# Preparing DMA-transposed pairs on GpSimd, two pairs ahead, and storing 128 rows in one DMA

## The chip, the cores and the metric

The kernel runs on one core of one Trainium2 chip. The metric is the device time of one execution in microseconds (us). Before the change it is 434.28 us (median; 434.15 to 434.98). Times of a kernel and of the kernel before are taken in the same rounds on the same chip. Engine names in the profile: PE is TensorE's matmuls, PEld its weight loads, DVE is VectorE, ACT ScalarE, POOL GpSimd, SP SyncE; SPq is SP's sequencer, which issues DMAs. A DMA has landed when its data have arrived. Tile names: `kst`, `qst` and `vst` are K, the queries and V as loaded, `kc` the copied K, `qp` the summed queries, `kT` and `qT` their transposes, `psc` the scores, `er` their exponentials, `xn` and `xT` the attention's output and its transpose, `osb` rows of the result before they are stored.

## The reference, cut to what matters

```python
def _attn_ref(q, k, v):                       # (8, 8, 1152, 64) each
    q_pool = q.reshape(B, H, S // 2, 2, D).mean(axis=3)
    attn = softmax(q_pool @ k.T / sqrt(D))    # 576 pooled queries, 1152 keys
    return attn @ v
# x = (batch, query) rows x 512 columns, 4608 rows
def _moe_ref(x, w1, w2, w3, w_out):           # 512 -> 1024 -> 1024 -> 512
    return ((x @ w1) * (x @ w2) @ w3) @ w_out
```

The kernel treats two heads of one batch as a "pair": 32 pairs in all. Pooling is a sum of two neighbouring queries; the half goes into the softmax scale. The feed-forward part runs in nine units of 512 rows; seven of them are mixed into the attention loop, the last two make the tail.

## The kernel before

Pairs 0 to 7 are transposed by PE. From pair 8 on, K and the summed queries are transposed by DMA, two pairs at a time. Each such turn has five steps: six cast loads (fp32 to fp16, issued by GpSimd), two K copies, one sum of queries, one transpose of K and one of the queries (issued by SP), and then `settled`: two tiny GpSimd copies that read the transposed tiles, so that GpSimd issues the next six loads only after the transposes have landed.

```python
    def load_two(P):
        load_k(P)
        load_q(P)
        load_q(P + 1)
        load_k(P + 1)
        load_v(P)
        load_v(P + 1)

    def pool_q(P, n=1):
        # ... (tile qp, slices)
        nc.vector.tensor_tensor(
            out=qps[pp][r].rearrange("p c u d -> p u c d"),
            in0=src[:, :, :, 0, :], in1=src[:, :, :, 1, :], op=ALU.add)

    def prep_dma(P):
        for p in (P, P + 1):
            new_kq(p)
            nc.vector.tensor_copy(out=new_kc(p).rearrange("p j u d -> p u j d"), in_=kst.pop(p))
        nc.sync.dma_start_transpose(
            out=kTs[P // 2].rearrange("p t j f -> p (t j) f"),
            in_=kc2[P // 2].rearrange("p t j u d -> p (t j u d)"))
        pool_q(P, 2)
        nc.sync.dma_start_transpose(
            out=qTs[P // 2], in_=qps[P // 2].rearrange("p c u d -> p (c u d)"))

    def settled(P):
        for n, t in enumerate((kT[P], qT[P])):
            nc.gpsimd.tensor_copy(out=seen[:, n:n + 1], in_=t[0:1, 0, 0:1])
```

The end of a group of 128 output rows. The row of `out` for a query is `9 p + c`, because queries are kept in the order (c, p), with p from 0 to 63; so 64 rows of the tile `osb` go to 64 rows of `out` that lie nine rows apart:

```python
            def end(p):
                if s == 0:
                    osbs[i] = ffp.tile([128, dm], FP32, tag="osb", bufs=3, name="osb")
                # ... (DVE, in the tail ACT, writes osb from the PSUM tile p)
                for z in range(2):
                    b, f = divmod(t0 + 128 * i + 64 * z, SQ)
                    dst = out[b * SQ:(b + 1) * SQ, :].rearrange("(p c) m -> c p m", c=NJ)
                    eng = nc.scalar if final and z else nc.sync
                    eng.dma_start(out=dst[f // 64][:, cs], in_=osbs[i][64 * z:64 * z + 64, cs])
```

And the scheduler, where `at` is the position in the loop, counted in pairs:

```python
        elif prepped < NP and at >= prepped - 1.25:
            prep_dma(prepped)
            if loaded < NP:
                settled(prepped)
                load_two(loaded)
                loaded += 2
            prepped += 2
```

The softmax here doesn't subtract the row's maximum and nothing guards it: scores larger than these inputs give would overflow.

## Time and profile before

| of before | value | view |
|---|---|---|
| device time | 434.28 us | times |
| PE busy | 94% of the span | first part of the page |
| last exponential starts | 370.1 us | trace, start times of the exponentials |
| from there to the end (tail) | 63.3 us | span less the line above |
| step of the loads' turn | 23.85 us per two pairs | trace, issue times of the load groups |

The page first: busy time and share of each engine, PE's busy tenths, the granted TensorE clock in tenths, the packets of SP's queue, and the shares of the chain of waits that ended last, by engine and by line.

```profile
span 433.4 us, 12640 instructions
PE 408.2 (94%) x5432; PEld 270.3 (62%) x5432; DVE 211.2 (49%) x442; ACT 326.4 (75%) x355; POOL 78.4 (18%) x135
...
PE   3999999999996999799999999899999999999995
...
PEclk9999999999999899899999999999999999999999
...
q1 hardware_dynamic: 67968, 24.66, 31.4%
...
PE 72%; DMA 10%; ACT 6%; SPq 4%; DVE 3%; issue 2%; POOL 1%; DVEq 0%; POOLq 0%; ACTq 0%
PE po L276 16%; PE psc L251 15%; PE pa L369 14%; PE pb L369 13%; PE pp L387 10%; ACT er L261 6%; DMA vst<-in_v_dram 5%; DMA qT<-qp 4%; PE pT L353 3%; SPq L140 3%; DMA kst<-in_k_dram 1%; SPq L304 1%; DVE kc L139 1%; POOL kst L88 1%; DVE gT L381 1%
```

PE is dense: only three of 40 slices, at about 130, 174 and 270 us, drop below nine tenths outside the ends. The DMA issues of the same page (issuing engine, count, KB each, median us from issue to landing):

```profile
qst<-in_q_dram POOLq DMA_DIRECT2D x32, 288.0 KB, 7.2
vst<-in_v_dram POOLq DMA_DIRECT2D x32, 288.0 KB, 11.1
out_dram<-osb SPq DMA_DIRECT2D x70, 128.0 KB, 3.5
kst<-in_k_dram POOLq DMA_DIRECT2D x31, 288.0 KB, 8.0
```

The waits of the engines (engine, tile, line, what ended the wait: us in total, times, longest):

```profile
POOL seen L149 <- DMA kT<-kc: 193.4, 11, 22.6
ACT er L261 <- PE psc L251: 55.6, 99, 3.2
...
DVE osb L399 <- DMA out_dram<-osb: 6.8, 2, 6.2
...
PE psc L251 <- DMA qT<-qp: 4.7, 4, 3.3
```

GpSimd waits for the transposed kT for 193 of the 433 us, and nobody minds: it has nothing else to do. But it means that the next loads are not issued until the transposes are there. The timeline at 136 us (start, length, engine, line) shows a place where PE itself has to wait for a transpose:

```profile
134.03 1.40 SPq L144 DMA_TRANSPOSE qT<-qp  x1
...
137.69 0.09 PEld L251 LDWEIGHTS <-kT 64*128 64x128 f16 x1 [1.80 <-DMA kT<-kc]
137.77 0.18 POOL L149 COPY seen<-kT 1x1 f16<-1x1 f16 x1 [22.61 <-DMA kT<-kc]
139.44 0.66 PE L251 MATMUL psc<-qT,kT 64*128 64x256 f16 x6 [3.25 <-DMA qT<-qp]
```

### The profile page before, as it was taken

How to read it: one execution, taken by the hardware profiler on the slowest of the kernel's cores; microseconds unless marked ns; L12 is line 12 of the kernel's file. 1: busy time of each engine (PE TensorE's matmuls, PEld its weight loads, DVE VectorE, ACT ScalarE, POOL GpSimd, SP SyncE). 2: the span in 40 equal slices, each digit the busy share in tenths (PEclk: the TensorE clock that was granted, in tenths of full speed). 3: DMA queues.
4: the chain of work that ended last, by engine and by line, in shares of the span. 5: the costliest groups of instructions: out<-in, count | busy, mean ns of one | idle time of the engine just before them, and what ended most of it. 6: DMA issues, size and time to landing. Idle time of an engine off the chain costs nothing.

```text
span 433.4 us, 12640 instructions
## 1 busy us (share of the span) xinstructions
PE 408.2 (94%) x5432; PEld 270.3 (62%) x5432; DVE 211.2 (49%) x442; ACT 326.4 (75%) x355; POOL 78.4 (18%) x135
## 2 busy tenths in 40 slices
PE   3999999999996999799999999899999999999995
PEld 1677777766773577566775577466766776544442
DVE  1455565646453563456455544555465535613140
ACT  4898899889886688689878888788888888233332
POOL 8433331030401304030403012303004000000000
PEclk9999999999999899899999999999999999999999
DMA  8999999898776959995796979996968662050404
GB/s 126 205 208 201 180 193 188 157 165 119 124 171 95 170 79 161 223 164 110 119 188 111 150 127 205 169 165 118 223 119 133 97 138 36 14 114 1 98 0 98
DMA packets 94729, 59.16 MB, mean 136 GB/s; under 512 B 65360, under 2 KB 85072, under 8 KB 94672
## 3 DMA queue, kind: packets, MB, share of 16 engines
q0 software_dynamic: 26544, 33.56, 48.1%
q1 hardware_dynamic: 67968, 24.66, 31.4%
q8 instruction: 42, 0.69, 0.7%
q10 hardware_dynamic: 160, 0.13, 0.1%
q14 instruction: 15, 0.12, 0.1%
HBM read 67.11 MB, written 9.44 MB: 177 GB/s over the span
## 4 chain that ended last, share of the span: by engine, by line
PE 72%; DMA 10%; ACT 6%; SPq 4%; DVE 3%; issue 2%; POOL 1%; DVEq 0%; POOLq 0%; ACTq 0%
PE po L276 16%; PE psc L251 15%; PE pa L369 14%; PE pb L369 13%; PE pp L387 10%; ACT er L261 6%; DMA vst<-in_v_dram 5%; DMA qT<-qp 4%; PE pT L353 3%; SPq L140 3%; DMA kst<-in_k_dram 1%; SPq L304 1%; DVE kc L139 1%; POOL kst L88 1%; DVE gT L381 1%
## 5 line engine op out<-in xcount | busy, mean ns | idle before, releaser
L261 ACT ACTIVATE er<-psc 128x1024 f16<-128x1024 f32 x324 | 307.8, 1025 | 55.9 <-PE psc L251 55.6
L276 PEld LDWEIGHTS <-er 128*128 128x128 f16 x2880 | 105.2, 98 | 23.8 <-issue 7.3
L276 PE MATMUL po<-vt,er 128*128 128x65 f16 x2880 | 112.5, 194 | 0.4 <-DVE xn L293 0.4
L251 PE MATMUL psc<-qT,kT 64*128 64x512 f16 (+7 forms) x1152 | 98.0, 290 | 13.5 <-DMA qT<-qp 4.7
L369 PE MATMUL pa<-xT,w1sb 128*128 128x512 f16 x288 | 75.7, 386 | 0.0
L381 DVE TENSOR_TENSOR gT<-pb,asb 128x512 f16<-128x512 f32 x72 | 49.8, 692 | 52.8 <-PE pb L369 51.5
L369 PE MATMUL pb<-xT,w2sb 128*128 128x512 f16 x288 | 74.5, 381 | 0.0
L251 PEld LDWEIGHTS <-kT 64*128 64x128 f16 x1152 | 46.4, 95 | 39.3 <-issue 17.7
L387 PE MATMUL pp<-T,gT 128*128 128x256 f16 (+1 forms) x488 | 67.9, 292 | 0.0
L387 PEld LDWEIGHTS <-gT 128*128 128x128 f16 x488 | 45.7, 98 | 18.5 <-issue 3.7
L379 DVE COPY asb<-pa 128x512 f32<-128x512 f32 x56 | 38.7, 690 | 35.5 <-PE pa L369 34.4
L369 PEld LDWEIGHTS <-w2sb 128*128 128x128 f16 x288 | 26.6, 98 | 33.4 <-issue 5.0
L369 PEld LDWEIGHTS <-w1sb 128*128 128x128 f16 x288 | 25.3, 99 | 30.6 <-issue 6.8
L399 DVE TENSOR_SCALAR osb<-pp 128x256 f32<-128x256 f32 x49 | 20.8, 425 | 40.5 <-PE pp L387 33.4
L149 POOL COPY seen<-kT 1x1 f16<-1x1 f16 x11 | 2.0, 178 | 193.4 <-DMA kT<-kc 193.4
L289 DVE RECIPROCAL rz<-po 128x5 f32<-128x5 f32 x64 | 12.4, 194 | 49.0 <-PE po L276 48.6
L293 DVE TENSOR_TENSOR xn<-po,rz 128x320 f16<-128x320 f32 x64 | 31.5, 492 | 2.2
L88 POOL DMA_DIRECT2D kst<-in_k_dram x33 | 24.2, 733 | 10.9 <-DMA kst<-in_k_dram 3.2
L95 POOL DMA_DIRECT2D vst<-in_v_dram x32 | 23.3, 741 | 12.1 <-DVE vt L133 3.3
L396 ACT ACTIVATE osb<-pp 128x512 f32<-128x512 f32 (+1 forms) x12 | 7.0, 580 | 24.2 <-PE pp L387 24.2
L377 ACT COPY asb<-pa 128x512 f32<-128x512 f32 x16 | 9.4, 586 | 16.4 <-PE pa L369 16.4
L80 POOL DMA_DIRECT2D qst<-in_q_dram x32 | 19.5, 615 | 9.9 <-DMA xT<-in_moe_w_out_dram 2.1
(39 smaller groups left out, 135.5 us busy)
## 6 DMA issues: line engine op xcount, KB each, us to landing
qst<-in_q_dram POOLq DMA_DIRECT2D x32, 288.0 KB, 7.2
vst<-in_v_dram POOLq DMA_DIRECT2D x32, 288.0 KB, 11.1
out_dram<-osb SPq DMA_DIRECT2D x70, 128.0 KB, 3.5
kst<-in_k_dram POOLq DMA_DIRECT2D x31, 288.0 KB, 8.0
w3h<-in_moe_w_dram POOLq DMA_DIRECT2D x4, 512.0 KB, 14.9
xT<-in_moe_w_out_dram POOLq DMA_DIRECT2D x2, 512.0 KB, 14.2
w1sb<-in_moe_w_dram POOLq DMA_DIRECT2D x2, 512.0 KB, 16.2
w2sb<-in_moe_w_dram POOLq DMA_DIRECT2D x2, 512.0 KB, 17.2
```

The source lines that it names most:

```text
L80: nc.gpsimd.dma_start(out=qst[P // 2][o:o + 64].rearrange("p u t d -> p u (t d)"), in_=q[b, h0:h0 + 2].rearrange("u (p t) d -> p u (t d)", ...
L88: nc.gpsimd.dma_start(out=kst[P][:, :, js[0]:js[1], :], in_=k[b, h0:h0 + 2].rearrange("u (p j) d -> p u j d", j=NJ)[:, :, js[0]:js[1], :])
L95: nc.gpsimd.dma_start(out=vst[P].rearrange("p u j d -> p u (j d)"), in_=v[b, h0:h0 + 2].rearrange("u (p j) d -> p u (j d)", j=NJ))
L251: nc.tensor.matmul(t[:, u, o:o + ln].rearrange("p (c f) -> p c f", f=64), kT[P][s, j, :], qT[P][s, f0 // 64:(f0 + ln) // 64], start=True, ...
L261: nc.scalar.activation(out=er[:, :, r:r + CH], in_=psc.pop(c), func=AF.Exp, bias=0.0, scale=SCALE)
L276: nc.tensor.matmul(po[P, u][:, VW * x:VW * x + D + 1], er[:, u, r:r + 128], vts[P % 4][:, u, j, 0:D + 1], start=(m == 0), stop=(m == 44), ...
L293: nc.vector.tensor_tensor(out=xn[:, P % 2, :, u, :], in0=acc[:, :, 0:D], in1=rz.to_broadcast([128, 5, D]), op=ALU.mult)
L369: nc.tensor.matmul(p, w[:, mc, ft * 128:ft * 128 + 128], xT[:, mc, t0:t0 + 512], start=(mc == 0), stop=(mc == NC - 1))
L379: nc.vector.tensor_copy(out=asb[ft], in_=p)
L381: nc.vector.tensor_mul(out=gT[:, ft, :], in0=p, in1=asb.pop(ft))
L387: nc.tensor.matmul(p[:, 0:n], gT[:, ft, 128 * i:128 * i + 128], T16[:, ft, n * s:n * s + n], start=(ft == 0), stop=(ft == NF - 1))
L399: nc.vector.tensor_scalar_mul(out=osb, in0=p[:, 0:n], scalar1=1.0 / (SCL * SCL))
```

## The change

Its intent: take the K copies and query sums off DVE, whose in-order stream stalls when a load is late; prepare earlier, at 1.95 pairs ahead instead of 1.25, so that transposes never come late; and halve the number of store issues. The diff, with some unchanged lines and the two transposes shortened (`...`); the loads of K also move behind those of Q and V, and the copy of V moves a little (1.2 to 1.1):

```diff
     def load_two(P):
-        load_k(P)
         load_q(P)
         load_q(P + 1)
-        load_k(P + 1)
         load_v(P)
         load_v(P + 1)
+        load_k(P)
+        load_k(P + 1)
 
     def pool_q(P, n=1):
 
+        eng = nc.gpsimd if n == 2 else nc.vector
         ...
-        nc.vector.tensor_tensor(
+        eng.tensor_tensor(
 
     def prep_dma(P):
 
+        pool_q(P, 2)
         for p in (P, P + 1):
             new_kq(p)
-            nc.vector.tensor_copy(out=new_kc(p).rearrange("p j u d -> p u j d"), in_=kst.pop(p))
+            nc.gpsimd.tensor_copy(
+                out=new_kc(p).rearrange("p j u d -> p u j d").bitcast(mybir.dt.int32),
+                in_=kst.pop(p).bitcast(mybir.dt.int32))
         nc.sync.dma_start_transpose(... kT <- kc)
-        pool_q(P, 2)
         nc.sync.dma_start_transpose(... qT <- qp)
 
                 cs = slice(n * s, n * s + n) if final else slice(0, dm)
+                b, f = divmod(t0 + 128 * i, SQ)
+                if f < SQ - 64 and not final:
+                    dst = out[b * SQ:(b + 1) * SQ, :].rearrange("(p c) m -> c p m", c=NJ)
+                    nc.sync.dma_start(out=dst[f // 64:f // 64 + 2], in_=osbs[i])
+                    return
                 for z in range(2):
 
-        elif prepped < NP and at >= prepped - 1.25:
+        elif prepped < NP and at >= prepped - 1.95:
-        if copied < NP and at >= copied - (1.2 if copied >= NPE else 0.6):
+        if copied < NP and at >= copied - (1.1 if copied >= NPE else 0.6):
```

Of the 36 groups of 128 rows, 31 become one store: 21 before the last exponential and 10 in the tail. The merged store's destination has the shape 2 x 64 x 512, its source 128 x 512.

## The prediction

> **What bounds it now.** The page shows PE busy 94% of the span; the chain of waits is 72% PE. Until 372 us the matmul order is fixed by the program and repeats every 27 iterations (8 pairs); each iteration starts with three exponentials of ACT. Laying the start times of the exponentials of the repeats over each other, nearly all iterations agree within 0.05 us; six do not: about +5.0 us at 136 us, +3.9 at 177, +2.4 at 270, +0.9 at 164 and two smaller, together about 13 us. The timeline shows why: at 136 us PE waits for the DMA-transposed kT and qT (issued only at 131-134 us, behind xT transposes on the SP queue); at 174-178 and 267-272 us DVE, in order, waits in its K copy and V copy for kst and vst loads, and with it the evictions that PE needs. After the first two PE ran at half clock for 3.4 us (clock record; counted in the 13). Nothing else is to be had: from 372 us on it is a dense PE tail.
>
> **What the change does.** (1) 24 K copies (0.45 us each) and 12 query sums (0.75 us) leave DVE, which is no bottleneck (49%). On GpSimd, the Trainium skill (GPSIMD Engine Reference, section 3.1) has about 2.6 cycles per element at 1.2 GHz for a two-input op: estimate 2.5 us per sum, about 0.6-0.9 us per copy; this trace shows no such GpSimd op. POOL has room (18% busy). (2) Preparation comes 0.7 pair (about 8 us) earlier, so kT, qT have about 22 us instead of 14. The late kT/qT (+5.9 us) and the DVE blocks (+6.3 us) should go: -12 us, to about 422, if nothing else changed. (3) The loop loads -> copies -> transposes -> loads is serial: about 13 us from load issue to last landing plus about 8 us of transposes and issue; its 21-22 us barely fit in the 22.6 us of two pairs.
>
> (4) The stores. Before: 64 rows, 128 KB, 16 engines, 2 KB packets of 96 ns each, 3.5 us to landing. After: the destination's outermost dimension is 2 (2x64x512), the source's 128. The Trainium skill (DMA: Bandwidth & Descriptors, "Why a DMA increments its semaphore by 16 and not by 1") says the transfer runs on the largest number of engines up to 16 that divides both outermost sizes: here 2. No trace yet shows it. Then a store is 64 packets on each of two engines: about 6 us, and stores serialize there. Estimate: 31 of them, 180-190 us on those two engines, which also carry a sixteenth of every load and transpose (about 8.5 + 5 us per two pairs). In a 46 us unit (4 stores) they need about 48 us: near saturation. Loads and transposes finish with their slowest engine, and transposes queue behind stores, so the loop of (3) lengthens: I guess +5 to +35 us before 372 us. Tail: four stores per 20.7 us, three buffers; ACT waits for a buffer (+3 to +5 us), and the last three stores, made 1.7 us apart, drain in about 18 us: end +11 us.
>
> **Sum.** -12 +15 (tail) +10 = 448 us; range 424 to 470. Faster by 2%: 0.18; within: 0.25; slower: 0.57.
>
> **What would show it.** Store landing 7 us or more (before 3.5); a wait of the tail's osb for out_dram; a chain ending in out_dram; the gaps of 136, 174 and 267 us gone; DVE busy down about 20 us; GpSimd sum near 2.5 us; kT/qT waits near the bursts of stores.
>
> **What would make it wrong.** If the stores use 16 engines, expect about 422 us (faster). If two engines have spare capacity, only the tail pays: about 436. If transposes stick behind stores, over 470.

## The result

The changed kernel takes 513.48 us (median; 513.17 to 518.54). Its time is 1.1847 times that of before, with a 95% interval of 1.1773 to 1.1921. A ratio here is always the mean time of one kernel's fast runs over that of the other's fast runs of the same rounds, so it is not quite the ratio of the medians quoted. The direction was predicted; the size was not: 513 lies far outside 424 to 470.

The page after, the same lines as above:

```profile
span 511.1 us, 12544 instructions
PE 425.4 (83%) x5432; PEld 276.5 (54%) x5432; DVE 197.0 (39%) x406; ACT 326.1 (64%) x355; POOL 122.5 (24%) x171
...
PE   4999999998895999493998849489996969979870
...
PEclk9999999999899899988899969879997989989995
...
q1 hardware_dynamic: 67038, 24.65, 35.9%
...
DMA 39%; PE 38%; SPq 7%; ACT 5%; POOL 5%; issue 3%; DVE 1%; POOLq 0%; DVEq 0%; ACTq 0%
DMA kst<-in_k_dram 20%; DMA out_dram<-osb 12%; PE pb L372 8%; PE pa L372 8%; PE psc L254 8%; PE po L279 8%; SPq L144 6%; DMA qT<-qp 5%; ACT er L264 5%; PE pT L356 3%; POOL vst L95 2%; POOL qst L80 2%; PE pp L390 2%; DMA kT<-kc 1%; POOL kc L141 1%
```

PE's row now has holes (the first wait of over 1.5 us is at 126 us), and the chain has turned from PE (72% to 38%) to DMA (10% to 39%). Two of its links have grown most: the loads of K, from 1% to 20%, and the stores, from less than 1% to 12%. PE's busy time rose by 17 us with the same 5432 matmuls; the clock record has ten stretches at half clock between 129 and 457 us, 61 us together, each beginning in a wait of PE or within 2 us of its end. The Trainium skill, "TensorE: Matmul & The Clock Gate", table in "Part 1: The HAM clock gate (the "warmup" mystery)", puts half clock after an idle window of about 3.4 us. The longest waits of PE here are longer than that (9.2 us, in the list below), so I read the lower clock as a consequence of the waits, not as their cause. With the same program and 64-row stores (first experiment) the mean clock is 0.999; with nothing but idle work added to that (e12_loop5), which makes PE wait, it falls to 0.970.

The line of q1 is the most useful of the page. SP's queue moved the same bytes in 67968 - 67038 = 930 packets fewer. Nothing moved to GpSimd was on that queue; only the stores changed. The Trainium skill, "DMA: Bandwidth & Descriptors", section "Why a DMA increments its semaphore by 16 and not by 1", says that each engine which takes part in a store posts one increment of its own. Before, 31 pairs of stores posted 31 x 2 x 16 = 992 of these. 992 - 930 = 62 are left, which is 2 for each merged store. The records of single packets agree: 4-byte packets on this queue fell from 3456 to 2526, and of the 2 KB packets never more than two were in flight for 188 of the 207 us in which there were any (before, more than eight for 30 of 64 us). So a merged store does run on two engines. In the tail three stores, 384 packets, took 16.9 us, thus 5.6 us a store; the prediction had estimated 6.

The issues and the waits after:

```profile
qst<-in_q_dram POOLq DMA_DIRECT2D x32, 288.0 KB, 6.9
vst<-in_v_dram POOLq DMA_DIRECT2D x32, 288.0 KB, 11.1
kst<-in_k_dram POOLq DMA_DIRECT2D x31, 288.0 KB, 15.0
out_dram<-osb SPq DMA_DIRECT2D x31, 256.0 KB
```

```profile
ACT er L264 <- PE psc L254: 116.3, 100, 8.8
POOL kc L141 <- DMA kst<-in_k_dram: 88.2, 22, 11.1
POOL seen L152 <- DMA kT<-kc: 70.0, 11, 13.0
POOL qp L121 <- DMA qst<-in_q_dram: 60.2, 12, 13.5
...
DVE osb L402 <- DMA out_dram<-osb: 42.5, 6, 9.9
...
PE psc L254 <- DVE osb L402: 26.0, 5, 9.2
...
DVE xn L296 <- DMA xT<-xn: 18.8, 3, 8.8
```

ACT waits 61 us longer for scores. PE waits five times for DVE, which waits six times for one of the three `osb` tiles to be stored (42.5 us; before 6.8). One of these places in the timeline:

```profile
239.60 0.66 POOL L141 COPY kc<-kst 128x576 int32<-128x576 int32 x1 [5.77 <-DMA kst<-in_k_dram]
242.23 0.42 DVE L402 TENSOR_SCALAR osb<-pp 128x256 f32<-128x256 f32 x1 [9.55 <-DMA out_dram<-osb]
242.36 0.66 POOL L141 COPY kc<-kst 128x576 int32<-128x576 int32 x1 [2.10 <-DMA kst<-in_k_dram]
242.71 0.61 PE L254 MATMUL psc<-qT,kT 64*128 64x128 f16 x4 [8.74 <-DVE osb L402]
...
243.05 2.71 SPq L144 DMA_TRANSPOSE kT<-kc  x1
243.25 1.41 PEld L390 LDWEIGHTS <-gT 128*128 128x128 f16 x8 [0.41 <-issue]
243.25 1.89 PE L390 MATMUL pp<-T,gT 128*128 128x256 f16 x8
243.41 1.02 ACT L264 ACTIVATE er<-psc 128x1024 f16<-128x1024 f32 x1 [7.63 <-PE psc L254]
```

Read it from the inner end: DVE idles 9.55 us for a store, PE 8.74 us for DVE, ACT 7.63 us for PE, and in the same stretch GpSimd waits for its K loads, so the K transpose is issued late, at 243 us.

Where the time is. The last exponential starts at 431.0 us (before 370.1), so 61 us of the difference lie in the loop; the tail is 80.1 us (before 63.3), 16.8 us more.

### The profile page after: what moved, and what is told of

It reads as the page before. It is cut to its first block, busy times and chain, and to the rows that moved or that the text cites. A ratio compares the mean times of both kernels' runs of the same rounds, so it can differ in the third digit from the quotient of the medians.

```text
span 511.1 us, 12544 instructions
## 1 busy us (share of the span) xinstructions
PE 425.4 (83%) x5432; PEld 276.5 (54%) x5432; DVE 197.0 (39%) x406; ACT 326.1 (64%) x355; POOL 122.5 (24%) x171
## 3 DMA queue, kind: packets, MB, share of 16 engines
q1 hardware_dynamic: 67038, 24.65, 35.9%
## 4 chain that ended last, share of the span: by engine, by line
DMA 39%; PE 38%; SPq 7%; ACT 5%; POOL 5%; issue 3%; DVE 1%; POOLq 0%; DVEq 0%; ACTq 0%
DMA kst<-in_k_dram 20%; DMA out_dram<-osb 12%; PE pb L372 8%; PE pa L372 8%; PE psc L254 8%; PE po L279 8%; SPq L144 6%; DMA qT<-qp 5%; ACT er L264 5%; PE pT L356 3%; POOL vst L95 2%; POOL qst L80 2%; PE pp L390 2%; DMA kT<-kc 1%; POOL kc L141 1%
## 5 line engine op out<-in xcount | busy, mean ns | idle before, releaser
L279 PE MATMUL po<-vt,er 128*128 128x65 f16 x2880 | 114.9, 196 | 22.3 <-DVE xn L296 14.1
L279 PEld LDWEIGHTS <-er 128*128 128x128 f16 x2880 | 107.1, 99 | 41.2 <-DVE xn L296 18.1
L254 PE MATMUL psc<-qT,kT 64*128 64x512 f16 (+7 forms) x1152 | 102.1, 300 | 30.9 <-DVE osb L402 26.0
L372 PE MATMUL pb<-xT,w2sb 128*128 128x512 f16 x288 | 78.9, 397 | 10.6 <-issue 6.4
L254 PEld LDWEIGHTS <-kT 64*128 64x128 f16 x1152 | 47.7, 97 | 66.7 <-issue 46.8
L372 PE MATMUL pa<-xT,w1sb 128*128 128x512 f16 x288 | 78.0, 395 | 0.0
L390 PE MATMUL pp<-T,gT 128*128 128x256 f16 (+1 forms) x488 | 71.6, 303 | 0.0
L390 PEld LDWEIGHTS <-gT 128*128 128x128 f16 x488 | 47.4, 101 | 21.4 <-issue 5.3
L402 DVE TENSOR_SCALAR osb<-pp 128x256 f32<-128x256 f32 x49 | 20.6, 424 | 76.2 <-DMA out_dram<-osb 42.5
L121 POOL TENSOR_TENSOR qp<-qst 128x1152 f16<-128x1152 f16 x12 | 28.2, 2354 | 60.2 <-DMA qst<-in_q_dram 60.2
L296 DVE TENSOR_TENSOR xn<-po,rz 128x320 f16<-128x320 f32 x64 | 31.5, 492 | 20.9 <-DMA xT<-xn 18.8
L141 POOL COPY kc<-kst 128x576 int32<-128x576 int32 x24 | 15.8, 662 | 88.2 <-DMA kst<-in_k_dram 88.2
## 6 DMA issues: line engine op xcount, KB each, us to landing
vst<-in_v_dram POOLq DMA_DIRECT2D x32, 288.0 KB, 11.1
w1sb<-in_moe_w_dram POOLq DMA_DIRECT2D x2, 512.0 KB, 15.9
```

Source lines behind the costliest of these rows:

```text
L121: eng.tensor_tensor(out=qps[pp][r].rearrange("p c u d -> p u c d"), in0=src[:, :, :, 0, :], in1=src[:, :, :, 1, :], op=ALU.add)
L254: nc.tensor.matmul(t[:, u, o:o + ln].rearrange("p (c f) -> p c f", f=64), kT[P][s, j, :], qT[P][s, f0 // 64:(f0 + ln) // 64], start=True, ...
L279: nc.tensor.matmul(po[P, u][:, VW * x:VW * x + D + 1], er[:, u, r:r + 128], vts[P % 4][:, u, j, 0:D + 1], start=(m == 0), stop=(m == 44), ...
L296: nc.vector.tensor_tensor(out=xn[:, P % 2, :, u, :], in0=acc[:, :, 0:D], in1=rz.to_broadcast([128, 5, D]), op=ALU.mult)
L372: nc.tensor.matmul(p, w[:, mc, ft * 128:ft * 128 + 128], xT[:, mc, t0:t0 + 512], start=(mc == 0), stop=(mc == NC - 1))
L390: nc.tensor.matmul(p[:, 0:n], gT[:, ft, 128 * i:128 * i + 128], T16[:, ft, n * s:n * s + n], start=(ft == 0), stop=(ft == NF - 1))
```

## The experiments

Two theories at the start. The theory of the stores: the loss is the merged stores' two engines, which lengthen each turn of loads, copies and transposes, and hold `osb` tiles. The theory of GpSimd: the loss is the chain of copies and sums, now on GpSimd, with the loads issued behind them by the same engine. Further rivals came up on the way: that two engines simply have no capacity for the work; that the size of a store counts and not its engines; that three `osb` buffers are too few; that stores block transposes in SP's queue; that `settled` makes the loop too tight.

Two numbers are read from every trace besides the time: the last exponential, and the step of the loop, which is the mean distance between two groups of loads on GpSimd (11 groups from 80 us on, one for each of 11 turns, so the mean is over 10 distances).

### e1_stores64: GpSimd part alone

```diff
 (after)
-                b, f = divmod(t0 + 128 * i, SQ)
-                if f < SQ - 64 and not final:
-                    dst = out[...].rearrange("(p c) m -> c p m", c=NJ)
-                    nc.sync.dma_start(out=dst[f // 64:f // 64 + 2], in_=osbs[i])
-                    return
```

> The changed kernel with its stores of 64 rows again (two DMAs a tile, as before the change); everything else of the change stays. Theory A (the merged stores run on two DMA engines, and all of the loss comes from that): 418 to 427 us, the gaps of before at 136, 177 and 270 us gone, no wait of osb for out_dram over 1 us in the attention part. Rival C (the serial loop of loads, GpSimd copies and transposes does not fit into two pairs, or GpSimd is too slow for the copies): still 450 us or more, with kT late.

Measured: correct, 424.49 us, ratio to before 0.9765 (0.9716 to 0.9813). This is within the expected range and faster than both kernels (against before it is clear of no change, but its interval reaches into 2%). The theory of GpSimd falls. Its waits and issues show what 64-row stores leave:

```profile
POOL seen L152 <- DMA kT<-kc: 58.7, 11, 6.6
...
POOL kc L141 <- DMA kst<-in_k_dram: 47.0, 22, 4.4
ACT er L264 <- PE psc L254: 46.1, 97, 1.8
```

Of PE's waits for a transpose one of 0.4 us is left, and GpSimd's wait for a K load is at most 4.4 us (after: 11.1). One detail of the expectation missed: `osb` still waits for stores three times before the last exponential, 2.1 us at most. The step is 22.41 us, the last exponential 360.7 us, and the tail 63.1 us, as before.

### e2_rows128: one store for 128 rows, but on 16 engines

```diff
 (after)
-                    dst = out[...].rearrange("(p c) m -> c p m", c=NJ)
-                    nc.sync.dma_start(out=dst[f // 64:f // 64 + 2], in_=osbs[i])
+                    t = t0 + 128 * i
+                    nc.sync.dma_start(out=out[t:t + 128, :], in_=osbs[i])
```

The rows land in the wrong order; the bytes, the number of stores and the packet size stay.

> The changed kernel, its merged stores kept at 128 rows and 256 KB in one DMA, but written to 128 consecutive rows of the output (wrong rows on purpose), so that the outermost size of the destination is 128 and no longer 2. Theory A: as fast as with stores of 64 rows, 418 to 427 us; the 2 KB packets of a store are up to 16 in flight. Rival B (one DMA of 256 KB is what hurts, by its size or by its later landing, whatever its shape): about 513 us.

Measured: wrong, 427.68 us (one of the four runs is a slow one; the fast ones are 422.67 to 428.76), ratio 0.9768 (0.9684 to 0.9852), as expected.

```profile
out_dram<-osb SPq DMA_DIRECT2D x31, 256.0 KB, 2.5
```

The page's packet count of SP's queue is 67472, which is 496 = 31 x 16 below that of before: 16 increments for each store instead of 32. So a store of 128 rows costs nothing by itself: it lands in 2.5 us, and the kernel is as fast as e1. Neither one large DMA nor holding `osb` until 256 KB have gone is the cause. The shape of the destination is.

### e3_before_merged: the merged stores alone

```diff
 (before)
                 cs = slice(n * s, n * s + n) if final else slice(0, dm)
+                b, f = divmod(t0 + 128 * i, SQ)
+                if f < SQ - 64 and not final:
+                    dst = out[...].rearrange("(p c) m -> c p m", c=NJ)
+                    nc.sync.dma_start(out=dst[f // 64:f // 64 + 2], in_=osbs[i])
+                    return
```

> The kernel before, with nothing changed but the merged stores. Theory A: slower by the tail (+15 to +18 us) and by osb, xn and kT waits before 372 us (+30 to +60 us): 480 to 515 us, perhaps worse than the changed kernel, as kT is prepared 8 us later. Rival C (the GpSimd loop makes most of the loss): at most 455 us, the tail alone.

Measured: correct, 514.59 us, ratio 1.1843 (1.1784 to 1.1902), the same as the whole change. The step is 29.72 us, the last exponential at 431.8 us. The merged stores alone make the whole loss; the GpSimd part, worth 2.3% with 64-row stores, is worth nothing beside them.

### e4_k8 and e5_k4: eight and four engines

```diff
 (after, e4_k8; e5_k4 likewise with 4 x 32 rows)
-                    nc.sync.dma_start(out=dst[f // 64:f // 64 + 2], in_=osbs[i])
+                    c0, x = f // 64 % 2, f // 128
+                    nc.sync.dma_start(out=dst[c0:c0 + 8, 16 * x:16 * x + 16], in_=osbs[i])
```

Wrong rows again; only the outermost size of the destination is meant to count.

> The changed kernel with its merged stores written as 8 x 16 rows (wrong rows on purpose; same bytes, same 2 KB rows, same number of DMAs), so that 8 divides both outermost sizes. Theory A: 8 engines, 16 packets each, about 1.4 us of engine time a store: 418 to 430 us, 1 to 4 us above the contiguous rows. Rival D (a destination in several strided blocks is slow whatever its outermost size): about 513 us.

> The changed kernel with its merged stores written as 4 x 32 rows (wrong rows on purpose, same bytes). Theory A (number of engines): 4 engines, 32 packets each, between the 442 us of 8 engines and the 513 us of 2: 455 to 480 us. Increments on the SP queue: 31 x 4 + 31 less per store than with 16, so 12 a store fewer. Rival (a threshold, something else breaks only at 2): at most 445 us.

Measured: e4_k8 441.86 us, ratio 1.0171 (1.0123 to 1.022); e5_k4 490.98 us, ratio 1.1264 (1.1163 to 1.1366). Both above their expected ranges. The packet counts of SP's queue are 67224 and 67100, below before by 31 x 24 and 31 x 28: 8 and 4 increments a store, as the rule for the number of engines has it. The order is right (16, 8, 4, 2 engines: 427.7, 441.9, 491.0, 513.5 us), but the loss over e2, 14, 63 and 86 us, is not in proportion to the time that a store keeps each engine (5.6 us on two, so about 1.4 and 2.8 us on eight and four): four engines already cost nearly three quarters of what two cost.

### e6_buffers: more buffers

```diff
 (after)
-            xns[P // 2] = ab.tile([128, 2, 5, 2, D], FP16, tag="xn", bufs=2, name="xn")
+            xns[P // 2] = ab.tile([128, 2, 5, 2, D], FP16, tag="xn", bufs=4, name="xn")
-                    osbs[i] = ffp.tile([128, dm], FP32, tag="osb", bufs=3, name="osb")
+                    osbs[i] = ffp.tile([128, dm], FP32, tag="osb", bufs=6, name="osb")
```

> The changed kernel, stores still on two engines, but six osb buffers in place of three and four xn buffers in place of two. If the stalls before 430 us come from buffers that wait for their store or their transpose to land (osb and xn waits make about 52 of some 70 us of excess in the trace), time falls to 440 to 465 us; the tail keeps the drain of its last stores. If the two engines are simply out of capacity (my prediction reckoned 48 us of work in 46 us), it stays above 490 us, the waits moving to kT and kst.

Measured: correct, 509.41 us, ratio 1.1699 (1.1612 to 1.1786). Only 4 us are won, although the waits named first are gone from the list of waits (of `osb` 1.0 us is left). That is the second branch of the expectation, no capacity:

```profile
ACT er L264 <- PE psc L254: 114.2, 99, 11.3
POOL kc L141 <- DMA kst<-in_k_dram: 88.5, 22, 13.6
...
PE psc L254 <- DMA qT<-qp: 26.1, 8, 7.1
```

ACT waits as long as ever and PE now waits 26.1 us for the transposed queries, as long as it had waited for DVE's `osb`. The `osb` waits in the timeline above are real, but behind them stands a loop that would have been late anyway: the step is 28.41 us (after 28.07). This is the case of a visible wait that is not the bound.

### e7_actq: merged stores from ACT's queue

```diff
 (after)
-                    nc.sync.dma_start(out=dst[f // 64:f // 64 + 2], in_=osbs[i])
+                    nc.scalar.dma_start(out=dst[f // 64:f // 64 + 2], in_=osbs[i])
```

> The changed kernel with its merged stores issued from ACT in place of SP, still on two engines but on another queue of them, so that transposes no longer stand behind store packets in the same queue, and stores no longer stand behind a kT transpose that waits for its K copy. If the order within the queue makes the loss: 445 to 475 us, xn and kT waits gone, osb waits small. If the occupancy of the two engines makes it: 495 us or more.

Measured: correct, 501.19 us, ratio 1.1529 (1.1458 to 1.1599). That is again the second branch of the expectation. If transposes had merely stood behind stores in one queue, this would have cured them. It made them worse and the loads better:

```profile
POOL seen L152 <- DMA kT<-kc: 109.9, 11, 20.3
...
POOL kc L141 <- DMA kst<-in_k_dram: 51.4, 22, 7.1
```

The step is 28.62 us. The wait moved from the loads (88.2 to 51.4 us) to the K transposes (70.0 to 109.9 us). The order within SP's queue decides who pays, and accounts for little of the sum.

### e8_dve_early: early, but on DVE, with 64-row stores

```diff
 (e1)
-        eng = nc.gpsimd if n == 2 else nc.vector
+        eng = nc.vector
-            nc.gpsimd.tensor_copy(
-                out=new_kc(p).rearrange("p j u d -> p u j d").bitcast(mybir.dt.int32),
-                in_=kst.pop(p).bitcast(mybir.dt.int32))
+            nc.vector.tensor_copy(
+                out=new_kc(p).rearrange("p j u d -> p u j d"), in_=kst.pop(p))
```

> The kernel with stores of 64 rows (424.5 us), early preparation kept, but K copies and query sums back on DVE. The trace of that kernel shows POOL waiting up to 9 us for Q and 4 us for K at this point; on DVE, which evicts PSUM in order, those waits stop PE: 440 to 470 us, slower than before. Rival (the earlier start alone makes the gain, the engine is indifferent): 422 to 428 us.

Measured: correct, 431.87 us, ratio 0.992 (0.9834 to 1.0006); the expectation missed, being too high, and so did its rival (422 to 428). DVE with its earlier place loses nothing; it just gains little.

### e9_pool_late: on GpSimd, but late, with 64-row stores

```diff
 (e1)
-        elif prepped < NP and at >= prepped - 1.95:
+        elif prepped < NP and at >= prepped - 1.25:
```

> The kernel with stores of 64 rows (424.5 us), copies on GpSimd, but preparation at the old place in the program (1.25 pairs ahead in place of 1.95). GpSimd runs nothing else, so only the place of kT among the transposes and stores of SP changes: kT stands behind later xT transposes and stores. If the early place is needed: 427 to 435 us, with kT waits at 136 us. If leaving DVE is all that matters: 422 to 426 us.

Measured: correct, 433.8 us, ratio 1.0033 (0.9961 to 1.0105), as expected. So with 64-row stores the four corners are: DVE late (before) 434, DVE early 432, GpSimd late 434, GpSimd early 424.5 us. Neither half of the GpSimd part gives its gain alone. The corners are not quite clean: the three new ones have the new order of loads and the new place of the V copy, and before has the old ones; no run tests these two alone.

### e12_loop5: 5.3 us of idle work in each turn of the loop

```diff
 (e1)
+    junk = const.tile([128, 2, 576], mybir.dt.int32)
+    nc.vector.memset(junk, 0)
                 settled(prepped)
+                for _ in range(8):
+                    nc.gpsimd.tensor_copy(out=junk[:, 1], in_=junk[:, 0])
                 load_two(loaded)
```

Here nothing of the DMA changes: the loop of loads and transposes is only made longer.

> The kernel with stores of 64 rows (424.5 us) and nothing slow on the DMA engines, but eight idle copies of 0.66 us (5.3 us) put on GpSimd before each set of loads, so that only the loop loads, copies, transposes, loads gets longer (22.4 us a turn in the trace, of 11 turns). Theory L (the loop has no slack against two pairs, so that every microsecond of it is paid 11 times): about 27.7 us a turn and 465 to 485 us. Rival (the loop has slack, and the merged stores hurt through the waits of osb and xn): at most 435 us.

Measured: correct, 458.71 us, ratio 1.058 (1.0529 to 1.0632). The step grew by 3.3 us, from 22.41 to 25.7, since shorter waits took back 2 of the 5.3 us; the last exponential moved by 33.6 us. 11 turns times 3.3 us are 36 us. The time is below the expected range, because the loop did have about 2 us of slack a turn. What the slack does not take up is paid in each of the 11 turns.

### e11_k2_free and e13_s64_free: without `settled`

```diff
 (after for e11_k2_free, e1 for e13_s64_free)
             if loaded < NP:
-                settled(prepped)
                 load_two(loaded)
```

The loads then need not wait for the transposes.

> The changed kernel, stores on two engines, but without the two tiny copies by which GpSimd waits for the transposes before it issues the next loads; loads follow the K copies at once, so a turn of the loop is loads and copies alone, 28.1 - 8 = about 20 us by the trace, under two pairs. Theory L: most of the loss before 430 us goes, 450 to 475 us is left (osb waits and the tail of 17 us). Rival (the two engines have no capacity for the work, whatever the order): 495 us or more.

> The same without that wait, with stores of 64 rows (424.5 us). With no other limit the 10 us of excess over the best iterations should shrink: 415 to 421 us. If loads that run beside transposes slow the transposes, 424 to 430 us.

Measured: e11_k2_free is correct and took 526.57 us (median; 520.71 to 533.25; the fast runs alone 1.2018 times before, 1.1936 to 1.21). e13_s64_free is correct and took 437.7 us, ratio 0.9991 (0.9914 to 1.0069). Both profiles fell in runs labelled slow, over 1.5% above the fastest run of their kernel, so I use them only for what is large. Theory L missed in e11_k2_free, and its rival's range (495 us or more, no capacity) was met; in e13_s64_free both ranges were missed. By the fast runs the merged stores cost as much without `settled` (1.2018 - 0.9991 = 0.203) as with it (1.1847 - 0.9765 = 0.208), so the loss does not depend on loads that wait for transposes. Without `settled`, the loads run beside the transposes, and these suffer: in the slow profile of e13_s64_free kT lands 14.7 us after the transpose is issued (median), against 4.7 in e1 with `settled`, and the waits of GpSimd begin with

```profile
POOL kc L141 <- DMA kT<-kc: 71.5, 7, 14.5
```

So `settled` is not an idle brake. It makes the loop serial, but parallel DMAs are no faster here: without it the fast runs of e13_s64_free are at 0.9991, those of e1 at 0.9765.

### e14_tail_only and e15_loop_only: which of the merged stores cost

```diff
 (after; e15_loop_only has `not tail`)
-                if f < SQ - 64 and not final:
+                if tail and f < SQ - 64 and not final:
```

> The changed kernel with merged stores only after the last exponential. If the two parts of the loss add and do not touch each other, the time before the last exponential is that of the kernel with 64-row stores (360.7 us) and the tail that of the changed kernel (80.1): 441 us, range 437 to 445. Rival: the tail is long because the stores of the loop leave a backlog; then it is 63 to 68 us and the time 424 to 430.

> The changed kernel with merged stores only before the last exponential. If the parts add: 431.0 + 63.3 = 494 us, range 488 to 500. Rival (backlog carried into the tail): 505 us or more.

Measured: e14_tail_only is correct, 440.1 us, ratio 1.0123 (1.0093 to 1.0152), as expected. e15_loop_only is correct, 503.05 us, ratio 1.1553 (1.1519 to 1.1587), 3 us above its range. The lines of the issues show that the split is what was meant:

```profile
out_dram<-osb SPq DMA_DIRECT2D x50, 128.0 KB, 3.2
out_dram<-osb SPq DMA_DIRECT2D x10, 256.0 KB
```

```profile
out_dram<-osb SPq DMA_DIRECT2D x21, 256.0 KB
out_dram<-osb SPq DMA_DIRECT2D x28, 128.0 KB
```

The last exponential is at 359.6 us in the first and at 438.4 us in the second; the tails are 78.2 and 63.0 us. The parts add: above e1's ratio, 1.0123 - 0.9765 = 0.036 and 1.1553 - 0.9765 = 0.179 make 0.215, and the whole change has 1.1847 - 0.9765 = 0.208. In time, about 16 us in the tail and 78 us in the loop. There is no backlog that the loop hands to the tail.

### e16_half_rows: two engines, half the bytes

```diff
 (after)
-                    nc.sync.dma_start(out=dst[f // 64:f // 64 + 2], in_=osbs[i])
+                    nc.sync.dma_start(out=dst[f // 64:f // 64 + 2, :, 0:256], in_=osbs[i][:, 0:256])
```

> The changed kernel with the merged stores of only the first 256 columns: packets of 1 KB, wrong on purpose (half of the output of these rows is not written), and still 2 increments for each store. If what costs is the time in which a store keeps its few engines busy, it is halved, as with four engines, and the time is near that of four engines: 491 us, range 475 to 500, with a tail of 66 to 72 us. If it is the number of engines alone, whatever they move: 505 us or more. If the cost is in the packets' count[...] and not in their bytes, also 505 or more.

Measured: wrong, 468.2 us (461.54 to 468.88), ratio 1.068 (1.0591 to 1.0769); the profiled run, at 468.68 us, is just over the line that makes it a slow one. This is below the expected 475 to 500. Still two increments a store (the packet count of SP's queue is 67038 again), half of the bytes, and (468.2 - 424.5) / (513.5 - 424.5) = 0.49 of the loss (two of the four runs are slow ones; by the ratios of the fast runs 0.44). So it is not the number of engines as such, nor the count of packets, which is unchanged. The loss goes with the bytes that the two engines carry.

### The loop, in one table

Means over ten turns of each trace, from the issue of the first load to the start of the second K copy, from the end of that copy to the first tiny copy of `settled` (kT has landed), and the step. The last two columns are measured against e1: the last exponential's shift, and 11 times the longer step.

| kernel | loads to 2nd K copy, us | to kT landed, us | step, us | last exponential, us | shift, us | 11 x step, us |
|---|---|---|---|---|---|---|
| e1_stores64 (16 engines) | 14.3 | 5.4 | 22.41 | 360.7 | 0 | 0 |
| e14_tail_only | 14.3 | 5.4 | 22.34 | 359.6 | -1 | -1 |
| e4_k8 | 15.8 | 5.1 | 23.81 | 373.4 | 13 | 15 |
| e16_half_rows (slow run) | 17.7 | 5.3 | 25.59 | 400.4 | 40 | 35 |
| e12_loop5 | 12.6 | 5.2 | 25.7 | 394.3 | 34 | 36 |
| e5_k4 | 18.8 | 5.4 | 26.86 | 413.3 | 53 | 49 |
| after (2 engines) | 19.0 | 6.5 | 28.07 | 431.0 | 70 | 62 |
| e6_buffers | 20.0 | 6.1 | 28.41 | 428.8 | 68 | 66 |
| e7_actq | 15.2 | 10.5 | 28.62 | 420.9 | 60 | 68 |

The step predicts the shift within about 8 us in every row. This alone does not say which causes which, since a late PE would also space the loads out; e12_loop5, where the loop was lengthened on purpose, and e6_buffers, where the waits for `osb` were taken away, give the direction. Three rows left out fit less well: e15_loop_only 78 us of shift for 68, e3_before_merged 71 for 80, and e8_dve_early 8 for -1, whose loss is not in this step. In the changed kernel the single loads-to-copy times are 13.5, 14.9, 25.8, 14.5, 25.5, 17.8, 21.1, 18.5, 25.1 and 13.2 us: not all loads are slower, but some take about 25 us where e1 has 15.9 at most.

The semaphore records of the traces, which the views above do not print, say more. Each load of K, Q or V posts 16 increments when it lands (I give those of one semaphore to its loads in order of issue). After 80 us the changed kernel has 66 such loads. In 22 of them 14 increments come first and then, after a gap of at least 1.5 us, the last two, up to 8.1 us later; in 12 others two come first and 14 after such a gap. In e1_stores64 and e14_tail_only, whose loop stores on 16 engines, no load has such a gap; before, e2_rows128, e8_dve_early, e9_pool_late and e12_loop5 have at most three, none after the 2nd or the 14th. In e5_k4, with stores on four engines, the gap lies after the 12th increment in 11 loads and after the 4th in 16. (e13_s64_free, in its slow profile, has 13 gaps at six places, six of them after the 14th.) So the loads split into as many engines as the stores use and the rest.

## Why the prediction was wrong

- **Two engines for a merged store, about 6 us each: right.** 62 increments for 31 stores; 5.6 us measured.
- **"-12 us, to about 422, if nothing else changed": right in size.** e1 is exactly this and measured 424.5 us. The split was not: the prediction added a gain of the early place (5.9 us) and one of leaving DVE (6.3 us), but e8_dve_early and e9_pool_late, with one of the two each, are at 0.992 and 1.0033, and only both together give 0.9765. Nor is it a plain term of a sum: beside merged stores it is worth nothing (e3_before_merged against after), perhaps because the early place only helps while the loop can keep up (not tested).
- **GpSimd op costs: right.** 2.354 us for a sum (estimated 2.5), 0.662 us for a copy (0.6 to 0.9). DVE's busy time fell by 14 us, not 20.
- **"+15 (tail)": right.** 16.8 us, and 15.6 us where only the tail's stores are merged (440.1 against 424.5).
- **"I guess +5 to +35 us before 372 us", entered as +10: this step failed.** It measured 70 us (431.0 - 360.7, after against e1), and 78 us with the merged stores of the loop alone. With it the sum comes out: 434 - 10 + 17 + 70 = 511 us. The other two terms were right within 2.3 us each, so this term is the whole of the miss.

Why it failed can be told from the prediction's own text. It saw that the 21 to 22 us of loads, copies and transposes "barely fit in the 22.6 us of two pairs", and that the two engines would be "near saturation". It then guessed a number instead of multiplying: a loop with so little slack pays its lengthening at each of its 11 turns. e12_loop5 shows the multiplier without touching any DMA. That the merged stores do their harm through this loop alone is argued and not shown: e11_k2_free, made to test it, went against its forecast. The lengthening itself, 28.07 - 22.41 = 5.7 us a turn, is about the engine time of one merged store, and about two such stores (21 in 11 turns) come in each turn; I don't offer this as a law, since with four engines the turn grew by 4.5 us and a store takes about 2.8. With hindsight, the prediction's own 6 us for a store, once in each of 11 turns, would have given an estimate of 66 us in place of the guess.

The exit named in the prediction ("if transposes stick behind stores, over 470") is not the cause either. Taking the stores off SP's queue left 501 us. The loads and the transposes both pay, whichever meets the stores.

What stays open:

- That the loads wait for the packets of stores on two shared engines rests on four things: the loss goes away with 16 engines, about halves with half of the bytes, shows up in the loads of another queue, and the increments of these loads split 14 and 2, or 12 and 4 with four engines. The trace does not name the engine of a packet, so that the late two are the stores' two is not shown. The Trainium skill (the section named above, "How many engines (k)") says that these DMAs use the lowest-numbered engines, thus the same two each time; no run here shows which.
- Whether the two engines are out of capacity, or only late in a serial loop, is not separated. The ranges for no capacity were met in e6_buffers, e7_actq and e11_k2_free. An estimate from the packet records: in e1 the packets of loads and transposes take about 18.4 us a turn on each engine (mean of 16, over nine turns), and the store packets of the changed kernel 24.6 us a turn, or 12.3 on each of two; these two would need 30.7 us in a turn of 28.1. Packets of one engine may overlap, so this proves nothing, but the prediction's 48 us of work in 46 us pointed the same way.
- Why four engines (491 us) cost more than two with half of the bytes (468 us), though a store keeps each engine as long in both, is not settled. The sum over the busy engines (11 against 6 us a store) fits the order of these two, but eight engines have the same 11 us and cost only 442.
- Two of the holes of the changed kernel (about 323 and 386 us) have no releaser in the trace, and I did not find their cause. A hint: PE goes on at 333.7 and 390.1 us, each time some 2.5 us after a 16 KB packet of the queue that the profile calls `instruction` (331.1 and 387.6 us, the first for over 21 us). PE may have waited for its own instructions; no run tests it.

## What to carry to other kernels

Before merging two stores into one, look at the outermost size of both access patterns: the Trainium skill's "DMA: Bandwidth & Descriptors", section "Rules for kernel authors", asks for a multiple of 16 there, and this case shows the price of a 2 (513 against 428 us for the same bytes in the same number of stores). After such a change, count the packets of the queue in the profile: the increments tell how many engines each DMA used. And where a change lengthens a serial loop of loads, copies and transposes, find its slack first, then multiply what is left over by the number of turns; a wait that looks large in the list (here `osb`) may only stand in front of that loop.

## What the Trainium skill lacked or had wrong

- "DMA: Bandwidth & Descriptors", "Why a DMA increments its semaphore by 16 and not by 1": its rule for the number of engines was right in every case tried: 16, 8, 4 and 2 increments a store (496, 744, 868 and 930 packets fewer than with 62 stores of 16). It doesn't say what a narrow DMA costs other traffic on the core; here, 31 stores of 256 KB: 428, 442, 491 and 513 us for the whole kernel with 16, 8, 4 and 2 engines.
- The same page, "Rules for kernel authors", says that a transpose next to ordinary DMAs needs nothing. That holds for results (e11_k2_free and e13_s64_free are correct), but the time is missing: beside cast loads the K transpose landed 14.7 us after its issue (median), against 4.7 us with the loads held back (a slow run of e13_s64_free against e1).
- The same page has no measured figure for a store's landing by its number of engines: 256 KB landed in 2.5 us on 16 (median, e2_rows128) and kept two engines busy for 5.6 us (tail of the changed kernel).
- "GPSIMD Engine Reference", "3.1 Elementwise — side-by-side cycle accounting": about 2.6 cycles per element gave an estimate of 2.5 us for the sum of 1152 fp16 values per partition; 2.354 us was measured, so it agrees within 6%. It has no figure for a strided copy as 32-bit words: 0.662 us for 576 words per partition.
